# Cosformer attention and a token/channel mixer: first batch's u products moved two to three channel steps forward, one sine on ScalarE, half of a transpose copied

## The chip, the cores and the metric

The kernel runs on one core of a Trainium2 chip. The metric is device time in microseconds (us), the median of several runs. Five engines work beside each other, each in the order of its own instructions: TensorE (PE in the profile; its weight loads are PEld), VectorE (DVE), ScalarE (ACT), GpSimd (POOL) and SyncE (SP), which here only issues DMAs. An engine waits for another by a semaphore.

## The reference

For 8 batches, 8 heads, 576 positions and a head dimension of 64, the attention takes the positive part of q and k, multiplies each with the cosine and with the sine of its position's angle, and joins the two into 128 features. With these

```
kv  = sum over s of k_p[s,f] * v[s,d]          (per head)
z   = sum over s of k_p[s,f]
x   = (q_p @ kv) / (q_p . z + 1e-6)
```

The result, as x of shape 8 x 576 x 512, goes through a mixer:

```
h   = relu(x^T @ w_tok1) @ w_tok2              (over tokens, 576 -> 256 -> 576)
u   = x + h^T
out = u + relu(u @ w_ch1) @ w_ch2              (over channels, 512 -> 1536 -> 512)
```

Inputs and output are in 32 bits; products are taken in bf16.

## The kernel before

The 576 positions of a batch are four full chunks (0 to 3) of 128 rows and a tail of 64 rows, chunk `R` = 4. The tails of two batches share one tile of 128 rows: the even batch has rows 0 to 63, the odd batch rows 64 to 127 (`self.rows`).

A batch has a front and a channel part. The front (class `Front`) makes the features of k and q (`feature`, L246 to L264: relu of the input times cosine or sine, for 8 heads at once, on VectorE at L263 or on ScalarE at L261), copies v to bf16 (`values`, L276 or, on ScalarE, L274), sums kv (`kv`, L321), transposes q's features (`q_trans`, eight 128 x 128 transposes on TensorE and one copy of the result out of PSUM on ScalarE, L345; later batches use DMA transposes), forms x (`num`, L360 to L370), the token products (`tok1`, L383) and u (`tok2`: a pair of products of 512 columns at L407 and VectorE's add of x at L410).

The channel part (class `Channel`) has twelve steps `c_main` of four products of 512 columns (L552), each followed by an activation on ScalarE (L556), then the steps of the output, `o_step` (L585, two products of 512 columns each; the add at L590 and the store by SP follow when a chunk is full).

The loop at the end runs the steps of batch b's channel part, and between them the pieces of the next front. Which piece comes after which step is written out by hand: `pieces` returns a plan of (step, function, arguments), sorted by step, and pieces of one step stay in their order in the list. Nothing is rearranged later: each engine gets its instructions in this order. `KS` and `QS` in the plan are the cosine and the sine feature of a chunk of k or q (a last `True` puts the sine on ScalarE), `V` the copy of v, `KV` the kv products, `QT` the transposes of q, `N` is `num`, `u` is `tok2` of the batch before. `O` = 12 is the first output step.

The change is in the plan of batch 1 (`first`), whose pieces run between the channel steps of batch 0. Batch 0's u isn't needed for its channel steps: for this batch the turned u is made directly, and steps 0 to 2 have run already in `first_front` (L562), so that plan entries for steps 3 to 11 follow one `c_main` each. Its u is needed for the adds of the output steps, and its tail for the channel steps of the next batch.

GpSimd has, in this stretch, the copies of v's chunks 2 and 3, and three issues of the loads of `w_ch2` (`load_w_ch2`, L196) between and after them. The first output step needs the first third of `w_ch2`.

PSUM has two pools: `ps_mm`, four buffers of one bank, for the channel and output products among others, and `ps_at`, two buffers of two banks. A product into a buffer waits for the reader of what was there.

Of the kernel before, what the change touches and what calls it, by code (L numbers as in the profile page):

```python
# [16 lines left out]
def kernel(  # L17
# [15 lines left out]
    nc = tc.nc  # L33
# [7 lines left out]
    R = S // P  # L41
# [31 lines left out]
    ps_at = ctx.enter_context(tc.tile_pool(name="ps_at", bufs=2, space=bass.MemoryType.PSUM))  # L73
# [142 lines left out]
    class Front:  # L216
# [119 lines left out]
        def q_trans(self, ci, heads=(0, H), eng=nc.scalar, pool=ps_mm):  # L336
            lo, hi = heads
            qT_ps = pool.tile([P, hi - lo, P], BF16, name="qT_ps",
                              tag="mm" if pool is ps_mm else "at")
            for h in range(lo, hi):  # L340
                nc.tensor.transpose(qT_ps[:, h - lo, :],  # L341
                                    self.q_of(ci)[:, h, :, :].rearrange("p a b -> p (a b)"), ident)
            dst = self.qpT[:, ci * H + lo:ci * H + hi, :] if ci < R else self.tail.qpT[:, lo:hi, :]
            if eng is nc.scalar:
                nc.scalar.copy(dst, qT_ps)  # L345
            else:
                nc.vector.tensor_copy(dst, qT_ps)
# [114 lines left out]
        def pieces(self, b, before):  # L462

            first, odd, late = b == 1, b % 2 == 1, b == 2
            V, KV, N = self.values, self.kv, self.num
            KS, QS, QT, T = self.k_side, self.q_side, self.q_trans, self.tok2
            C, O = 0, NCH
            if first:  # L470

                u, act, pool = before.tok2, nc.scalar, nc.gpsimd
                plan = [(4, KS, 0), (4, KS, 1), (5, u, 0, ps_at, False), (5, KS, 2, True),
                        (6, KS, 3, True), (6, u, 1, ps_at, False), (7, KS, R), (7, V, R, nc.vector), (8, V, 0, act),
                        (8, V, 2, pool), (8, load_w_ch2, 0), (8, V, 3, pool),
                        (8, load_w_ch2, 1), (8, load_w_ch2, 2),
                        (8, u, 2, None, False), (9, V, 1, act), (9, u, 3, None, False),
                        (9, QS, 0), (10, u, R, None, False)]
                plan += [(11, KV, ci) for ci in range(NSC)]
                plan += [(11, QS, 1), (11, QS, 2), (11, self.kv_out),  # L480
                         (11, QT, 0, (0, H), act, ps_at), (11, QT, 1), (11, QS, R),
                         (O, QT, 2), (O, N, 0), (O, QS, 3), (O + 1, QT, R),
                         (O + 1, N, 1), (O + 3, N, 2), (O + 3, QT, 3),
                         (O + 5, N, R), (O + 7, N, 3), (O + 8, before.tail_cast)]
            else:
                if late:
                    plan = [(C + 5, V, 1, nc.vector), (C + 5, V, 3, nc.vector),
                            (C + 6, V, 0, nc.scalar), (C + 6, V, 2, nc.scalar),
                            (C + 7, V, R, nc.scalar)]
                else:  # L490
                    plan = [(C + at, V, ci, nc.scalar)
                            for ci, at in enumerate((-1, -1, 0, 1, 2))]

                if odd:
                    sides = ((-4, KS, 0), (-3, QS, 0), (0, KS, 1), (0, KS, 2), (1, QS, 1),
                             (1, KS, 3), (1, QS, 2), (2, QS, 3))
                elif late:
                    sides = ((-4, KS, 0), (-3, KS, 1), (0, KS, 2), (1, KS, 3), (1, QS, 0),
                             (2, QS, 1), (3, QS, 2), (4, QS, 3), (5, KS, R), (9, QS, R))
                else:  # L500
                    sides = ((-4, KS, 0), (-3, KS, 1), (0, KS, 2), (1, KS, 3), (1, QS, 0),
                             (2, KS, R), (2, QS, 1), (3, QS, 2), (4, QS, R), (5, QS, 3))
                for at, side, ci in sides:
                    plan.append((C + at, side, ci))
                    if side == QS:
                        plan.append((C + at, self.q_trans_dma, ci))

                plan += [(C + at, KV, ci) for ci, at in
                         enumerate((7, 7, 8, 8, 8) if late else
                                   (2, 3, 4, 5, 6) if odd else (2, 3, 4, 6, 7))]  # L510
                plan.append((C + (8 if late else 6 if odd else 7), self.kv_out))
            if first:
                at, mix, t = (), O + 7, O + 11
            elif odd:
                at, mix, t = (C + 8, C + 9, C + 10, C + 11, O + 2), O + 3, O + 7
            elif late:
                at, mix, t = (C + 10, C + 11, O + 1, O + 2, O + 4), O + 5, O + 9
            else:
                at, mix, t = (C + 9, C + 10, C + 11, O + 1, O + 3), O + 4, O + 8
            plan += [(i, N, ci) for i, ci in zip(at, ORDER)]  # L520
            plan += [(mix, self.mix_head, 0), (mix + 1, self.mix_head, 1),
                     (mix + 2, self.mix_tail)]

            plan += [(t + at, T, ci) for ci, at in enumerate((0, 1, 2, 3, 3) if not first else
                                                             (0, 0, 1, 2, 2))]
            plan += [(t + 3 - first, self.u_trans_dma, 3, R)]
            plan.append((t + 2 - first, self.u_trans_dma, 0, 3))
            if odd:
                plan.append((t + 3 - first, self.tail_trans_dma))
            slots = {}  # L530
            for slot, what, *args in sorted(plan, key=lambda p: p[0]):
                slots.setdefault(slot, []).append((what, args))
            return slots
# [281 lines left out]
```

## Time and profile before

| what | value |
|---|---|
| median of 3 runs | 268.99 us (268.74 to 269.48) |
| profiled execution | 268.4 us |
| its span | 266.6 us, 1.8 us less than its time |
| granted TensorE clock | 1.00 |
| busy TensorE, VectorE, ScalarE, GpSimd | 260.2, 166.1, 127.5, 12.3 us |
| channel steps 3 to 11 of batch 0 | 26.70 to 36.84 us |
| GpSimd in this stretch | 32.38 to 35.93 us |
| first output product (L585) | 38.96 us |

The span is what the profile shows, from the first to the last instruction; the time also holds what lies around it. Start times below are in us from the span's start. Matmuls are pipelined: a product's row is longer than the distance between two starts, and that distance, the pitch, is what tells whether TensorE waits. Features on VectorE overlap in the same way.

### The profile page before, as it was taken

Reading aid. Unit: us, or ns where it says so; the run is one execution under the profiler, and the core shown is the slowest. Engines: PE = TensorE matmul, PEld = TensorE weight load, DVE = VectorE, ACT = ScalarE, POOL = GpSimd, SP = SyncE. Lnnn points to the kernel's source line nnn. Section 1 sums busy time; section 2 is a strip of 40 time slices with the busy share of each in tenths; the row PEclk is TensorE's granted clock in tenths of the full one; section 3 lists DMA queues with packets and bytes.
Section 4 is the critical chain, followed back from the end, with each engine's and each line's share of the span. In section 5 each row is a group of like instructions: output and inputs, shape, how many; then the busy total and the mean of one; then the engine's idle time right before and its main releaser. Section 6 shows DMA issues by size and latency. Waiting matters only on the chain.

```text
span 266.6 us, 5133 instructions
## 1 busy us (share of the span) xinstructions
PE 260.2 (98%) x2042; PEld 139.9 (52%) x2063; DVE 166.1 (62%) x381; ACT 127.5 (48%) x224; POOL 12.3 (5%) x26
## 2 busy tenths in 40 slices
PE   7999999999999999999999999999999999999995
PEld 3675466465644455446644455446644455445544
DVE  6974699785665946785565846876565846720022
ACT  4953976428515461646515462546516362516500
POOL 6410130000000000000000000000000000000000
DMA  6999999779998999459984989289974580180022
GB/s 218 331 285 270 331 165 239 277 191 300 172 373 247 293 194 340 111 154 267 178 299 121 294 218 350 65 179 241 242 252 118 157 121 0 50 208 2 2 89 107
DMA packets 91959, 53.68 MB, mean 201 GB/s; under 512 B 59424, under 2 KB 87072, under 8 KB 91936
## 3 DMA queue, kind: packets, MB, share of 16 engines
q1 hardware_dynamic: 88576, 49.62, 70.0%
q0 software_dynamic: 2832, 3.21, 7.3%
q10 hardware_dynamic: 528, 0.52, 0.6%
q8 instruction: 16, 0.26, 0.4%
q14 instruction: 7, 0.06, 0.1%
HBM read 35.85 MB, written 9.44 MB: 170 GB/s over the span
## 4 chain that ended last, share of the span: by engine, by line
PE 86%; DVE 9%; DMA 2%; issue 1%; DVEq 0%
PE o_ps L585 34%; PE c_ps L552 25%; PE b_ps L383 6%; PE u_ps L407 6%; PE ct_ps L572 4%; PE kv_ps L321 3%; PE num_ps L360 3%; DVE x_sb L370 3%; DVE qp L263 2%; DMA qt<-in_q_dram 2%; PE idle_ps L204 1%; PE c_ps L562 1%; DVE u_sb L410 1%; PE qT_ps L341 1%; DVE den L368 1%
## 5 line engine op out<-in xcount | busy, mean ns | idle before, releaser
L585 PE MATMUL o_ps<-w_ch,h1T 128*128 128x512 bf16 (+2 forms) x392 | 92.7, 366 | 0.6
L552 PE MATMUL c_ps<-uT,w_ch 128*128 128x512 bf16 (+2 forms) x384 | 91.9, 372 | 0.1
L556 ACT ACTIVATE h1T<-c_ps 128x512 bf16<-128x512 f32 x93 | 55.4, 598 | 60.0 <-PE c_ps L552 59.7
L585 PEld LDWEIGHTS <-h1T 128*128 128x128 bf16 x408 | 37.6, 98 | 39.4
L552 PEld LDWEIGHTS <-w_ch 128*128 128x128 bf16 x384 | 33.6, 97 | 29.8
L590 DVE TENSOR_TENSOR o_sb<-o_ps,u_sb 128x512 f32<-128x512 f32 (+2 forms) x34 | 22.4, 659 | 29.2 <-PE o_ps L585 27.2
L410 DVE TENSOR_TENSOR u_sb<-u_ps,x_sb 128x512 f32<-128x512 f32 x32 | 21.7, 689 | 5.8 <-PE u_ps L407 5.6
L414 ACT CAST u_bf<-u_sb 128x512 bf16<-128x512 f32 x28 | 17.2, 618 | 16.7 <-DVE u_sb L410 16.7
L407 PE MATMUL u_ps<-B,w_tok 128*128 128x512 bf16 x79 | 22.4, 379 | 0.2
L388 ACT ACTIVATE B<-b_ps 128x512 bf16<-128x512 f32 x8 | 4.8, 597 | 34.1 <-PE b_ps L383 34.1
L370 DVE TENSOR_TENSOR x_sb<-num_ps,den 128x512 bf16<-128x512 f32 x28 | 19.4, 691 | 1.0
L572 PEld LDWEIGHTS <-w_ch 128*128 128x128 bf16 x192 | 13.9, 98 | 8.7
L263 DVE TENSOR_SCALAR kp<-kt,cos_t 128x512 bf16<-128x512 f32 x32 | 15.2, 479 | 4.2 <-DMA kt<-in_k_dram 4.2
L383 PE MATMUL b_ps<-x_sb,w_tok 128*128 128x512 bf16 x63 | 17.7, 379 | 0.1
L572 PE MATMUL ct_ps<-uT_tail,w_ch 128*128 128x128 bf16 x192 | 16.9, 219 | 0.0
L263 DVE TENSOR_SCALAR qp<-qt,cos_t 128x512 bf16<-128x512 f32 (+1 forms) x35 | 15.8, 452 | 0.5 <-DMA qt<-in_q_dram 0.5
L263 DVE TENSOR_SCALAR qp<-qt,sin_t 128x512 bf16<-128x512 f32 (+1 forms) x35 | 15.8, 452 | 0.0
L274 ACT CAST v_aug<-vt 128x512 bf16<-128x512 f32 (+1 forms) x28 | 15.5, 584 | 0.1
L590 DVE TENSOR_TENSOR o_sb<-o_ps,u_tail 128x512 f32<-128x512 f32 x4 | 2.8, 692 | 19.0 <-PE o_ps L585 19.0
L332 DVE CAST kv_sb<-kv_ps 128x260 bf16<-128x260 f32 x8 | 3.4, 431 | 17.1 <-ACT kv_sb L332 15.9
L360 PEld LDWEIGHTS <-qpT 128*128 128x128 bf16 x256 | 11.5, 98 | 4.9 <-issue 0.7
L263 DVE TENSOR_SCALAR kp<-kt,sin_t 128x512 bf16<-128x512 f32 x28 | 13.4, 480 | 0.0
(94 smaller groups left out, 232.1 us busy)
## 6 DMA issues: line engine op xcount, KB each, us to landing
out_dram<-o_sb SPq DMA_DIRECT2D x31, 256.0 KB, 3.2
kt<-in_k_dram SPq DMA_DIRECT2D x7, 1024.0 KB, 6.9
vt<-in_v_dram SPq DMA_DIRECT2D x7, 1024.0 KB, 7.6
qt<-in_q_dram SPq DMA_DIRECT2D x7, 1024.0 KB, 9.1
w_ch<-in_moe_w_ch_dram POOLq DMA_DIRECT2D x4, 384.0 KB, 10.7
w_ch<-in_moe_w_ch_dram POOLq DMA_DIRECT2D x3, 512.0 KB, 8.0
out_dram<-o_sb SPq DMA_DIRECT2D x9, 128.0 KB, 2.3
qtt<-in_q_dram SPq DMA_DIRECT2D x8, 128.0 KB, 5.2
```

The lines of the kernel that those rows point to most:

```text
L263: nc.vector.tensor_scalar(o_ap, i_ap, scalar1=w, scalar2=0.0, op0=ALU.mult, op1=ALU.max)
L360: nc.tensor.matmul(num_ps[:, g, j * DP:j * DP + D1], self.qT_of(ci, h), self.kv_sb[g][:, j, 0:D1], start=True, stop=True)
L370: nc.vector.tensor_mul(self.x_of(ci)[rows].rearrange("p (g j d) -> p g j d", g=2, j=HH), nv[:, :, :, 0:D], den.to_broadcast([rows.stop - r ...
L383: nc.tensor.matmul(self.b1_ps[mi], w, self.x_of(ci), start=(ci == ORDER[0]), stop=(ci == ORDER[-1]))
L407: nc.tensor.matmul(u_ps, w_tok2[:, ki, ci * P:(ci + 1) * P], self.B1[:, ki, :], start=(ki == 0), stop=(ki == NT - 1))
L410: nc.vector.tensor_add(u, u_ps[rows], self.x_of(ci)[rows])
L414: nc.scalar.copy(self.ub[:, ci, :], u)
L552: nc.tensor.matmul(c_ps[:, lo:hi], w_ch1[:, ki, mi * P:(mi + 1) * P], uT[:, lo // P:hi // P, ki, :], start=(ki == 0), stop=(ki == NCC - 1))
L556: nc.scalar.activation(self.h1T[:, mi, :], c_ps, AF.Relu)
L572: nc.tensor.matmul(self.ct_ps[:, mi % R, :], w_ch1[:, ki, mi * P:(mi + 1) * P], self.tail.uT[:, ki, :], start=(mi % R == 0 and ki == 0), s ...
L585: nc.tensor.matmul(o_ps, h, w_ch2[:, ki, cols], start=ki == 0, stop=ki == NCH - 1)
L590: nc.vector.tensor_add(o_sb, o_ps, u)
```

## The change

In the plan of batch 1, the u products of batch 0's chunks 0 to 3 and their adds move from the places after steps 5, 6, 8 and 9 to those after steps 3, 4, 5 and 6, all four in `ps_at`; the tail's moves from step 10 to step 8, still in `ps_mm`. The k features of chunks 0 to 3 move behind the four u, from steps 4, 4, 5 and 6 to steps 6, 6, 6 and 7; the tail's k features move from step 7 to step 8. The sine of query chunk 2 goes to ScalarE. Apart from the plan, `q_trans` for the tail of an odd batch copies only the columns of that batch's 64 rows out of PSUM; the transposes are the same. GpSimd's and SP's instructions keep their order.

```
@@ q_trans
             dst = self.qpT[:, ci * H + lo:ci * H + hi, :] if ci < R else self.tail.qpT[:, lo:hi, :]
+            if ci == R and self.rows.start:
+                dst, qT_ps = dst[:, :, self.rows], qT_ps[:, :, self.rows]
             if eng is nc.scalar:
@@ pieces
                 u, act, pool = before.tok2, nc.scalar, nc.gpsimd
-                plan = [(4, KS, 0), (4, KS, 1), (5, u, 0, ps_at, False), (5, KS, 2, True),
-                        (6, KS, 3, True), (6, u, 1, ps_at, False), (7, KS, R), (7, V, R, nc.vector), (8, V, 0, act),
+                plan = [(3, u, 0, ps_at, False), (4, u, 1, ps_at, False), (5, u, 2, ps_at, False),
+                        (6, u, 3, ps_at, False), (6, KS, 0), (6, KS, 1), (6, KS, 2, True),
+                        (7, KS, 3, True), (8, u, R, None, False), (8, KS, R),
+                        (8, V, R, nc.vector), (8, V, 0, act),
                         (8, V, 2, pool), (8, load_w_ch2, 0), (8, V, 3, pool),
-                        (8, load_w_ch2, 1), (8, load_w_ch2, 2),
-                        (8, u, 2, None, False), (9, V, 1, act), (9, u, 3, None, False),
-                        (9, QS, 0), (10, u, R, None, False)]
+                        (8, load_w_ch2, 1), (8, load_w_ch2, 2), (9, V, 1, act), (9, QS, 0)]
                 plan += [(11, KV, ci) for ci in range(NSC)]
-                plan += [(11, QS, 1), (11, QS, 2), (11, self.kv_out),
+                plan += [(11, QS, 1), (11, QS, 2, True), (11, self.kv_out),
```

## The prediction

> **What bounds the kernel now.** I read the page's busy shares first, then the timeline of TensorE, VectorE and GpSimd around the edited steps, then the chain that ended last in that stretch.
>
> ```profile
> PE 260.2 (98%) x2042; PEld 139.9 (52%) x2063; DVE 166.1 (62%) x381; ACT 127.5 (48%) x224; POOL 12.3 (5%) x26
> ```
>
> A busy TensorE is not yet a TensorE at its peak, so its starts are compared next.
>
> ```profile
> 26.70 2.75 PE L552 MATMUL c_ps<-uT,w_ch 128*128 128x512 bf16 x12
> 29.29 0.38 PE L407 MATMUL u_ps<-B,w_tok 128*128 128x512 bf16 x1
> 29.72 1.03 PE L552 MATMUL c_ps<-uT,w_ch 128*128 128x512 bf16 x4
> ...
> 34.47 1.03 PE L552 MATMUL c_ps<-uT,w_ch 128*128 128x512 bf16 x4
> 35.55 0.59 PE L407 MATMUL u_ps<-B,w_tok 128*128 128x512 bf16 x2
> 35.98 1.02 PE L552 MATMUL c_ps<-uT,w_ch 128*128 128x512 bf16 x4
> 36.84 1.14 PE L321 MATMUL kv_ps<-v_aug,kp 128*128 128x65 bf16 x32
> 38.06 1.06 PE L341 MATMUL qT_ps<-ident,qp 128*128 128x128 bf16 x16
> 38.96 0.38 PE L585 MATMUL o_ps<-w_ch,h1T 128*128 128x512 bf16 x1
> ```
>
> Columns are start, duration, engine, line, operation, tiles, count. Twelve products in 2.59 us (26.70 to 29.29) are 0.216 each; a channel step (four) takes 0.864, a u pair 0.43 (29.29 to 29.72). Nine such steps and five pairs make 9.94, and 26.70 to 36.84 is 10.14: TensorE is fed without a break but for one hole of 0.2, ahead of the pair at 35.55, which a channel step from 34.47 would let start at 35.33. That pair reuses the PSUM bank of the u product whose add is the first of the two at 34.80, done at 35.49. (A count of 1 where the pitch says 2 is a missing record.) From 49 to 263 us the windows show it busy for 213.19 of 214.00. So moving its products can shorten the run by that 0.2 and little else, while a new wait lengthens it one to one.
>
> ```profile
> 32.44 0.83 DVE L263 TENSOR_SCALAR kp_tail<-ktt,cos_t 64x512 bf16<-64x512 f32 x1
> 33.20 0.83 DVE L263 TENSOR_SCALAR kp_tail<-ktt,sin_t 64x512 bf16<-64x512 f32 x1
> 33.95 0.82 DVE L276 CAST v_aug<-vtt 64x512 bf16<-64x512 f32 x1
> 34.80 1.29 DVE L410 TENSOR_TENSOR u_sb<-u_ps,x_sb 128x512 f32<-128x512 f32 x2
> ...
> 39.43 0.49 DVE L263 TENSOR_SCALAR qp_tail<-qtt,cos_t 64x512 bf16<-64x512 f32 x1
> ```
>
> ```profile
> 32.38 0.62 POOL L276 CAST v_aug<-vt 128x512 bf16<-128x512 f32 x1 [11.74 <-DMA vt<-in_v_dram]
> 32.94 0.77 POOL L196 DMA_DIRECT2D w_ch<-in_moe_w_ch_dram  x1
> 33.70 0.79 POOL L276 CAST v_aug<-vt 128x512 bf16<-128x512 f32 x1
> 34.44 1.49 POOL L196 DMA_DIRECT2D w_ch<-in_moe_w_ch_dram  x2
> ```
>
> ```profile
> 32.72 0.48 issue
> 33.20 0.21 DVE kp_tail L263
> 33.41 0.54 issue
> 33.95 0.82 DVE v_aug L276
> ```
>
> The same feature operation takes 0.49 at 39.43, with its successor 0.40 behind it, and 0.83 with a successor 0.76 behind it while GpSimd casts and issues its loads; the chain calls the excess "issue", a wait that no semaphore explains. The u adds (L410, from PSUM) keep 0.60 apart, also next to GpSimd's later issues. So VectorE's SBUF features pay 0.36 each (0.755 less 0.395) beside this GpSimd stretch. The Trainium skill (SBUF — State Buffer, "SBUF: two separate sides") says that the two engines share a port pair under an exclusive lock, held for a whole instruction, for VectorE's two-port modes; these rows agree, since the third operation ends 0.29 after the second cast (34.77 against 34.49).
>
> **The change, part by part.**
>
> *The u products.* The pairs of chunks 0 to 3 go behind channel steps 3, 4, 5, 6, and start at 27.56, 28.86, 30.15 and 31.45; that of the tail follows step 8, at 33.6. The stretch holds the same products, and the tail's pair no longer waits for an add, so the hole goes: step 11 could start at 35.77, 0.2 sooner. All four now use the two-buffer pool; each finds its buffer free, since the add of two pairs before ends 1.2 us earlier. Worth 0.2, if VectorE keeps up.
>
> *The adds.* VectorE can start one 0.63 after its pair's start (the o pair at 47.16, its add at 47.79). So the last of the four runs at 32.08 and frees VectorE at 32.69. VectorE was idle until 28.76 for k's load; the adds use 0.6 of that, but then wait 0.7 between each other for TensorE, and the eight k features (six on VectorE) are queued behind them, 28.76 becoming 32.69.
>
> *VectorE's queue from 32.69, nothing in its way.* Six features at 0.395: 35.06. The tail's add, 0.60: 35.66. Two tail features and the tail's cast at 0.40: 36.86. First query chunk, 0.79: 37.65; second: 38.44, done at 38.52; cosine of the third: 38.84. TensorE started query chunk 0 at 38.06 and chunk 1 at 38.51 and could now do so 0.2 sooner; chunk 1 would start at about 38.6, 0.1 later than before. The 0.2 is given back, and 0.1 with it.
>
> *The same queue beside GpSimd.* GpSimd's cast starts at 32.38, when v lands, before the first feature; the order of GpSimd is unchanged. So now three full features meet the cast, the issue and the second cast which three tail operations met before. I take their measured starts: 32.69, 33.20, 33.95, and the fourth at 34.69 where free running gives 33.88: 0.81 later. Two more GpSimd issues follow (34.44 to 35.93), next to which the trace has no feature. The nearest row is the issue of 32.94, during which the feature at 33.20 lost 0.36; the farther row is the four issues at 10.55 to 13.76, beside which features kept 0.40. I take 0.36 for each of the two, as the next features again come out of a block and alternate with GpSimd; bounds 0 and 0.72 together.
>
> *A new wait on TensorE.* In the built program channel step 11 takes the PSUM bank of the tail's u product, so it waits for that add, which stands behind all six features. Free running it ends at 35.74, in time for 35.77. With 0.81 it ends at 36.55, with 0.81 + 0.72 at 37.27: step 11 starts 0.6 or 1.3 later than at 35.98, and kv, the transposes and the first o products are queued behind it. That isn't added to the later wait: it only moves TensorE closer to it.
>
> *The sine moved to ScalarE.* It takes 0.395 off VectorE (counted) and puts 0.80 (the rows at 29.98) on ScalarE after its activation of 37.04 to 37.64, where it idled 0.63 before the kv copy at 38.26. That copy slips by 0.1 to 38.34 at most; its readers wait for VectorE's half at 38.98 anyway. 0.
>
> *Half of the tail's transposes copied.* 1.04 becomes about 0.6 (that line's smallest copies, 512 columns, start at 0.59). The copy ended at 42.47 and its reader started at 43.65; ScalarE then waited 0.52 for transposes. 0; nothing but that idle time grows.
>
> *SP and GpSimd queues* keep their order; q's load and the first third of w_ch2 keep their issue times.
>
> *Sum.* Query chunk 1 is ready at 38.52 + 0.81 + 0.72 = 40.05, and TensorE starts it at 40.1 in place of 38.51: 1.6 us late. Later readers (the kv copy, then the tail queries at 41.7 against 42.1) are in time. Nothing behind gives it back: the u sums, transposing DMAs and loads of the next batches are issued from what TensorE has done. The profiled execution took 268.4 with a span of 266.6, so 270.0 and 268.2. The median of the runs, 268.99, is 0.6 above it; I add to that: 270.6.
>
> **Rivals.**
>
> *The last two GpSimd issues don't hold VectorE* (for: the rows at 10.55; against: the one at 33.20). Only 0.81 remains: chunk 1 is ready at 39.33, started at 39.4, 0.9 late: 269.9.
>
> *VectorE isn't interrupted, and GpSimd starves instead.* The features then end at about 35.2 (blocked by the first cast only), and the first third of w_ch2 can be described only then rather than by 33.7. The shortest of its three loads took 5.9 from issue to landing, so it landed about 38.84, and the first o product starts at 38.96: no slack. It would land 1.5 late: 270.5. For: at 10.36 to 13.99 features ran at full pitch beside four issues, whose loads needed 10.7 to land against 8.0 here. Against: the first feature comes out of a block. The Trainium skill (SBUF — State Buffer, "SBUF: two separate sides", its box on VectorE blocking DMA) describes exactly this starving; the rows at 10.36 agree, those at 33.20 do not.
>
> *Not slower.* If GpSimd's casts fall elsewhere, or a full-height feature isn't held as the 64-row ones were, only the 0.1 stays: 269.1. It decides as long as the six features lose less than some 0.7 in all: below that the second query chunk is at most 0.8 late. For: no row shows a 128-row feature beside a GpSimd cast. Against: the rows at 32.44 to 34.77, and v's landing, which the change does not touch.
>
> *Faster, but hardly.* Were VectorE's features ready in time after all, the hole of 0.2 would be the whole gain, 268.8, which is inside what counts as same; more would need TensorE time that the change does not remove.
>
> **How the numbers follow.** A measurement of this kernel tells about 0.3% (0.8 us) from no change. Chances: forecast 0.45; the issues not holding 0.20; starving 0.12; not slower, the 0.2 gained among it, 0.20; faster by more 0.03. The second case lies at the boundary, so a third of it counts as same. Slower: 0.45 + 0.13 + 0.12 = 0.70; same 0.20 + 0.07 = 0.27; faster 0.03. The range runs from 269.1 (not slower) to 271.1: forecast plus 0.5, when a stall of GpSimd's own (each of its issues held up by a 0.27 feature) comes on top.
>
> **What would show it.** In the trace after: four L410 rows ahead of the first k feature, which starts near 32.7; several k features of 0.8 in place of 0.48 between 32.7 and 36; the first idle or stretched pitch of TensorE ahead of the last channel step (before: 35.98), then query chunk 1 near 40.1; from there every later start about 1.6 later than before, up to the end. k features at 0.48 throughout and an o product waiting for a DMA would speak for starving; step 11 at 35.8 and transposes by 38.1 would make the prediction wrong.

## The result, and the profile after

The changed kernel takes 270.46 us (median of 7 runs, 270.02 to 271.20) against 269.46 of the kernel before, run beside it: a ratio of 1.0045, 95% interval 1.0026 to 1.0063. It is slower, by 0.7 to 1.7 us. Twelve more runs on another occasion gave 270.45 against 269.17, 1.0050 (1.0032 to 1.0067). The profiled execution took 270.66 with a span of 268.5 (before: 268.4 and 266.6), at a granted clock of 1.00.

The busy shares have hardly moved: a loss of 0.4% cannot be found there.

```profile
PE 261.0 (97%) x2042; PEld 139.6 (52%) x2063; DVE 165.7 (62%) x380; ACT 127.4 (47%) x225; POOL 12.3 (5%) x26
```

The timeline of TensorE after, columns as before; what stands in brackets is the idle time ahead of the row and what ended it:

```profile
34.27 1.89 PE L554 MATMUL c_ps<-uT,w_ch 128*128 128x512 bf16 x8
36.80 1.02 PE L554 MATMUL c_ps<-uT,w_ch 128*128 128x512 bf16 x4 [0.64 <-DVE u_tail L412]
...
39.77 0.62 PE L341 MATMUL qT_ps<-ident,qp 128*128 128x128 bf16 x8 [0.17 <-DVE qp L263]
...
74.50 0.42 PE L362 MATMUL num_ps<-kv_sb,qpT_tail 128*128 128x65 bf16 x8 [0.36 <-DMA qpT_tail<-qp_tail]
```

The hole ahead of the tail's u pair is gone: steps 9 and 10 follow it at full pitch. In its place the last channel step waits for the tail's add, the second query chunk for its sine, and a third wait, which I had not forecast, stands almost 35 us later, ahead of the product at 74.50.

VectorE and GpSimd after:

```profile
32.92 0.53 DVE L263 TENSOR_SCALAR kp<-kt,cos_t 128x512 bf16<-128x512 f32 x1
33.37 0.82 DVE L263 TENSOR_SCALAR kp<-kt,sin_t 128x512 bf16<-128x512 f32 x1
34.11 0.72 DVE L263 TENSOR_SCALAR kp<-kt,cos_t 128x512 bf16<-128x512 f32 x1
34.76 0.47 DVE L263 TENSOR_SCALAR kp<-kt,sin_t 128x512 bf16<-128x512 f32 x1
35.15 0.99 DVE L263 TENSOR_SCALAR kp<-kt,cos_t 128x512 bf16<-128x512 f32 x2
36.06 0.68 DVE L412 TENSOR_TENSOR u_tail<-u_ps,x_tail 64x512 f32<-64x512 f32 x1
```

```profile
31.90 0.61 POOL L276 CAST v_aug<-vt 128x512 bf16<-128x512 f32 x1 [11.43 <-DMA vt<-in_v_dram]
32.46 0.76 POOL L196 DMA_DIRECT2D w_ch<-in_moe_w_ch_dram  x1
33.22 0.69 POOL L276 CAST v_aug<-vt 128x512 bf16<-128x512 f32 x1
33.87 1.66 POOL L196 DMA_DIRECT2D w_ch<-in_moe_w_ch_dram  x2
```

Read the starts, not the durations. Free, a feature follows the last one after 0.395. Here the distances are 0.45, 0.74, 0.65, 0.39 and, from 35.15 to the add at 36.06, 0.91 for two. The six take 3.14 in place of 2.37 and lose 0.77. The first is held by the end of GpSimd's first issue, the second by its second cast, the third by its second issue and the fifth by its third issue; the fourth runs free inside that third issue, and the sixth has nothing beside it. The chain of waits goes straight through them, and puts its only larger piece without a releaser between them:

```profile
32.31 0.69 DVE u_sb L412
33.01 1.50 DVE kp L263 x3
34.51 0.25 issue
34.76 1.39 DVE kp L263 x3
36.14 0.61 DVE u_tail L412
```

### The profile page after: what moved, and what is told of

It reads as the page before. It is cut to its first block, busy times and chain, and to the rows that moved or that the text cites. A ratio compares the mean times of both kernels' runs of the same rounds, so it can differ in the third digit from the quotient of the medians.

```text
span 268.5 us, 5134 instructions
## 1 busy us (share of the span) xinstructions
PE 261.0 (97%) x2042; PEld 139.6 (52%) x2063; DVE 165.7 (62%) x380; ACT 127.4 (47%) x225; POOL 12.3 (5%) x26
## 4 chain that ended last, share of the span: by engine, by line
PE 87%; DVE 8%; DMA 3%; issue 1%; ACT 0%; DVEq 0%
PE o_ps L587 33%; PE c_ps L554 26%; PE u_ps L409 6%; PE b_ps L385 6%; PE ct_ps L574 4%; PE kv_ps L321 4%; DVE x_sb L372 3%; PE num_ps L362 3%; DMA qt<-in_q_dram 2%; DVE qp L263 1%; PE idle_ps L204 1%; DVE kp L263 1%; DMA qpT_tail<-qp_tail 1%; PE qT_ps L341 1%; PE c_ps L564 1%
```

## The experiments

The kernel before ran beside each of them: 269.01 us beside `order_only`, `sine_copy`, `tail_bank` and `between` (34 runs), 269.01 again beside the next four (24 runs), and 269.17 beside `pe_hold` and `after_again` (23 runs). The diffs are cut to the lines that tell.

**Which part costs: the order alone, and the two small edits alone.** `order_only` is the changed kernel without the sine on ScalarE and the half copy; `sine_copy` is the kernel before with these two.

```
order_only, against the kernel after:
-                plan += [(11, QS, 1), (11, QS, 2, True), (11, self.kv_out),
+                plan += [(11, QS, 1), (11, QS, 2), (11, self.kv_out),
...
-            if ci == R and self.rows.start:
-                dst, qT_ps = dst[:, :, self.rows], qT_ps[:, :, self.rows]
```

> The new order of the u products and k features alone, with the sine of query chunk 2 on VectorE and the whole copy as before. Theory (VectorE's queue runs late because the k features stand behind four paced adds and beside GpSimd): the loss is all in the order, so about 1.0 to 1.5 us slower than before, within 0.4 of the changed kernel; channel step 11 waits near 36.8 for the tail's add, query chunk 1 starts near 39.8, and the third chunk's sine costs VectorE 0.4 more, which shows as a later kv copy. Rival (the sine on ScalarE, behind which the kv copy and the transposes' copies queue, is what costs): this kernel is within 0.3 us of before.

> The old order with only the sine on ScalarE and the half copy. Theory: within 0.3 us of before; VectorE reaches the kv copy 0.4 sooner, and nothing on TensorE waited for that; ScalarE's kv copy slips by 0.1. Rival (the sine on ScalarE costs): 1 us slower than before, with num waiting for ScalarE's copies.

Measured: `order_only` 270.11, ratio 1.0044 (1.0029 to 1.0058); `sine_copy` 269.25, ratio 1.0007 (0.9993 to 1.0021). The whole loss belongs to the new order; the two small edits are worth nothing that can be measured. In `order_only` the six features run from 32.98 to 36.37, 1.02 lost, step 11 starts at 37.09 after a wait of 0.88, and query chunk 1 at 40.07. In `sine_copy`, where k landed at 28.00 and not at 28.73, and v at 31.52 and not at 32.33, the hole of 0.2 is absent although the old order stands. It is absent in `pe_hold` below too, where k and v landed within 0.07 of before: the tail's pair starts at 35.48, right behind the step of 34.61. So the 0.2 that the change could have won stands in one of three profiles of the old order.

**Is it the PSUM bank?** `tail_bank` lets the tail's u pair use the other pool, so that step 11 need not wait for its add.

```
-                        (7, KS, 3, True), (8, u, R, None, False), (8, KS, R),
+                        (7, KS, 3, True), (8, u, R, ps_at, False), (8, KS, R),
```

> The changed kernel, with the tail's u product in the two-buffer pool, so that channel step 11 has no bank to wait for. Theory (the wait of step 11 only brings TensorE nearer to the wait for the query features): step 11 starts unhindered near 36.0 instead of 36.8, but query chunk 1 still starts near 39.8, since VectorE's queue is the same; time within 0.3 us of the changed kernel. Rival (the bank is the cause): 0.8 us of the loss comes back.

Measured: 270.53, ratio 1.0053 (1.0035 to 1.0072), no better than the change. Its TensorE:

```profile
34.20 2.75 PE L554 MATMUL c_ps<-uT,w_ch 128*128 128x512 bf16 x12
...
38.93 0.62 PE L341 MATMUL qT_ps<-ident,qp 128*128 128x128 bf16 x8 [0.52 <-DVE qp L263]
39.72 0.62 PE L341 MATMUL qT_ps<-ident,qp 128*128 128x128 bf16 x8 [0.17 <-DVE qp L263]
```

Twelve products without a break: step 11 no longer waits. The first query chunk does, for 0.52, and chunk 1 starts at 39.72 (after: 39.77). The wait named at step 11 is not the cause; VectorE's queue is, and the bank only decides where TensorE meets it.

**Is it the place of the features?** `between` keeps the early u pairs but puts the k features between their adds, ahead of GpSimd's stretch, and the tail's k features ahead of its u. The new lines of the plan:

```
+                plan = [(3, u, 0, ps_at, False), (4, KS, 0), (4, u, 1, ps_at, False), (5, KS, 1),
+                        (5, u, 2, ps_at, False), (6, KS, 2, True), (6, KS, 3, True),
+                        (6, u, 3, ps_at, False), (7, KS, R), (8, u, R, None, False),
                         (8, V, R, nc.vector), (8, V, 0, act),
```

> The changed kernel's early u products, but the k features between the adds, where VectorE waits for TensorE: u0, k chunk 0, u1, k chunk 1, u2, k chunks 2 and 3, u3. Theory: the full k features are done before GpSimd's casts start near 32 and keep their pitch of 0.40; only the tail's features meet the casts, as before; no wait for step 11 nor for the query chunks, and the hole of 0.2 before the tail's u pair is gone: 0 to 0.3 us faster than before, 1 us or more faster than the changed kernel. Rival (early products cost by themselves, by their buffers or by ScalarE's later activations): it stays as slow as the changed kernel.

Measured: 269.30, ratio 1.0013 (0.9997 to 1.0029). The loss is gone. VectorE:

```profile
29.02 0.48 DVE L263 TENSOR_SCALAR kp<-kt,cos_t 128x512 bf16<-128x512 f32 x1
29.41 0.48 DVE L263 TENSOR_SCALAR kp<-kt,sin_t 128x512 bf16<-128x512 f32 x1
...
31.80 0.87 DVE L263 TENSOR_SCALAR kp<-kt,cos_t 128x512 bf16<-128x512 f32 x2
```

The k features keep 0.40 from 29.02 to 32.6, and what meets GpSimd is again the 64-row tail (0.71 and 0.86). Faster than before it is not. The hole of 0.2 is gone, but the first output product could now start 0.06 sooner, at 38.90, and waits 0.18 for the first third of `w_ch2`, which landed at 39.04 (before: 38.87): the load had no slack. `between_load` issues that third ahead of GpSimd's casts, still only when v has landed.

```
-                        (8, V, 2, pool), (8, load_w_ch2, 0), (8, V, 3, pool),
+                        (8, load_w_ch2, 0), (8, V, 2, pool), (8, V, 3, pool),
```

> The kernel with the k features between the adds, and the first third of w_ch2 issued ahead of GpSimd's first cast instead of behind it. In the kernel without this its first o product waited 0.18 for that load. Theory: that wait goes, since the load is issued 0.5 sooner; no wait on TensorE from 26.7 to 44 over 0.1; 0 to 0.4 us faster than before, which is less than what the rounds can tell. Rival: the casts come later and the last chunks of kv wait for v.

Measured: 269.04, ratio 1.0008 (0.9993 to 1.0022). The load landed at 38.25 and the wait is gone; 0.2 us of TensorE is still too little to tell from no change. So neither version beats the kernel before.

**How much does GpSimd hold VectorE?** `issues_first` keeps the changed order, but has GpSimd issue its three loads first and cast afterwards; `no_pool_casts` also moves the two casts to ScalarE (and query chunk 2's sine back to VectorE), so that only issues are left beside the features; `no_pool_stretch` lets these issues go when k has landed, so that nothing is left beside them.

```
issues_first, against the kernel after (the first load waits for v):
-                        (8, V, 2, pool), (8, load_w_ch2, 0), (8, V, 3, pool),
-                        (8, load_w_ch2, 1), (8, load_w_ch2, 2), (9, V, 1, act), (9, QS, 0)]
+                        (8, load_w_ch2, 0), (8, load_w_ch2, 1), (8, load_w_ch2, 2),
+                        (8, V, 2, pool), (8, V, 3, pool), (9, V, 1, act), (9, QS, 0)]
no_pool_casts, against issues_first:
-                        (8, V, 2, pool), (8, V, 3, pool), (9, V, 1, act), (9, QS, 0)]
+                        (9, V, 1, act), (9, V, 2, act), (10, V, 3, act), (9, QS, 0)]
no_pool_stretch, against no_pool_casts: the first load waits for k in place of v
```

> The changed kernel, with GpSimd's three loads of w_ch2 issued first when v has landed (near 32), and its two casts of v after them (near 34 to 35.5). Theory A (casts and issues both hold VectorE's features): the features still lose some 0.8 in all, the first ones beside the issues at a pitch near 0.75, the later ones beside the casts; time within 0.4 us of the changed kernel. Theory B (only casts hold): pitch 0.40 up to about 34.1, then 0.7 for two or three features beside the casts; time 0 to 0.4 us better than the changed kernel. Rival (128-row features are slow at this place for a reason of their own): the same pitches at the same features as in the changed kernel, the second and third ones the slow ones.

> The changed kernel, with the casts of v's chunks 2 and 3 on ScalarE (after steps 9 and 10), the sine of query chunk 2 back on VectorE, and GpSimd left with the three issues alone, made when v has landed (near 32 to 34.2). Theory A (issues hold too): two features lose about 0.3 each instead of 0.8 in all; step 11 starts near 36.4 and query chunk 1 near 39.3; 0.3 to 0.6 us better than the changed kernel. Theory B (only casts hold): pitch 0.40 throughout, step 11 near 36.0 and query chunk 1 near 38.9; about 0.8 us better. Rival (GpSimd has nothing to do with it): features as slow as in the changed kernel, and no gain.

> As the kernel with GpSimd left with the issues alone, but they are made when k has landed (near 28.5 to 30.7), so GpSimd does nothing while the features run. Theory (the loss is the features' 0.8 beside GpSimd, and what the paced adds cost alone is 0.1): all six features at 0.40, the tail's add done near 36, step 11 not later than 36.1, query chunk 1 near 38.8, with at most 0.3 of waiting in all, unless v or q land later behind the earlier weights; time within 0.4 us of before. Rival (the four adds paced by TensorE cost most): step 11 still waits 0.5 or more.

Measured: 271.01, ratio 1.0082 (1.0064 to 1.0100), in 4 runs; 269.77, ratio 1.0033 (1.0017 to 1.0048), in 6; 270.07, ratio 1.0047 (1.0027 to 1.0068), in 9. VectorE in `issues_first`:

```profile
33.18 0.62 DVE L265 TENSOR_SCALAR kp<-kt,sin_t 128x512 bf16<-128x512 f32 x1
33.73 0.84 DVE L265 TENSOR_SCALAR kp<-kt,cos_t 128x512 bf16<-128x512 f32 x1
34.49 0.82 DVE L265 TENSOR_SCALAR kp<-kt,sin_t 128x512 bf16<-128x512 f32 x1
35.24 1.58 DVE L265 TENSOR_SCALAR kp<-kt,cos_t 128x512 bf16<-128x512 f32 x2
```

and in `no_pool_stretch`:

```profile
33.16 0.48 DVE L265 TENSOR_SCALAR kp<-kt,sin_t 128x512 bf16<-128x512 f32 x1
33.56 0.48 DVE L265 TENSOR_SCALAR kp<-kt,cos_t 128x512 bf16<-128x512 f32 x1
33.96 0.48 DVE L265 TENSOR_SCALAR kp<-kt,sin_t 128x512 bf16<-128x512 f32 x1
```

In the first, features and GpSimd's items alternate from 33.73 on, at 0.75 a feature, whether the item is an issue (until 35.04) or a cast: 1.57 lost, the most of all runs and twice what I expected. In the second every feature keeps 0.395 and nothing is lost.

The two kernels differ in more than GpSimd's work beside the features: the loads run earlier in the second, and ScalarE makes the casts. The ends of the single features settle which it is. Six profiles have k features of 128 rows beside GpSimd (after, `after_again`, `order_only`, `tail_bank`, `issues_first`, `no_pool_casts`). In them 23 features are held, and each ends 0.22 to 0.25 after the end of the issue beside it or 0.28 to 0.29 after the end of the cast beside it. Seven features run free inside an issue, and just these seven issues take 0.85 to 0.93, all others 0.75 to 0.77. So of a feature and an item side by side one waits for the other, and GpSimd's work is the cause.

`no_pool_casts` lies between: beside issues alone two of six features are held, by 0.14 each; step 11 starts at 36.17 and query chunk 1 at 39.14. That misses what I took for an issue, 0.36. The time of `no_pool_stretch` misses the 0.4 us of before within which I expected it, and decides nothing: step 11 waits for nothing there, but the loads let go earlier hold back those of the queries (VectorE waits 0.24 for the first, TensorE then 0.21 at query chunk 1 and 0.66 for the tail queries, whose load landed at 40.67), the kv products wait 0.43 for ScalarE's casts, and the late wait, of which more below, is at its largest, 1.24. It shows VectorE free, not what that is worth; that the time comes back with the features is shown by `between`.

**Is a delay given back, and what is the wait at 74.50?** `pe_hold` is the kernel before with six products of no use put ahead of the kv products (they also take a turn of `ps_at`'s two buffers); `after_again` is the changed kernel with a second profile.

```
+        def hold(self, times):
+            t = ps_at.tile([P, 2, 512], F32, name="hold_ps", tag="at")
+            busy(t[:, 0, :], times)
...
+                plan.append((11, self.hold, 6))
                 plan += [(11, KV, ci) for ci in range(NSC)]
```

> The kernel before, with nothing of the change, and six products of an identity by a 512-column operand of zeros (left unread) put on TensorE ahead of the kv products: 6 x 0.216 = 1.30 us of TensorE alone, at the place where the change delays it, while VectorE, ScalarE, GpSimd and the loads keep their times. My theory (a delay there lengthens the run one to one): kv at 38.1 in place of 36.84, query chunk 0 at 39.4, every later start 1.3 later, median about +1.3 (ratio 1.0045 to 1.005); no wait for the transposing DMA of the tail's queries near 73 us if that wait has its own cause in the loads, a wait of 0.4 or more there if it comes of the delay itself. Rival (something behind gives part of it back, an idle stretch or a clock effect): median +0.7 or less, ratio below 1.003.

> The changed kernel once more, unaltered, on the same chip and with a profile of its own. If its losses are the same from run to run: six k features of 3.1 to 3.4 us in all beside GpSimd, query chunk 1 about 1.0 to 1.6 later than in the kernel before, ratio 1.004 to 1.005; the wait for the transposing DMA near 74 us (0.36) present again. If that later wait is chance of one execution, it is absent and the last product lies 1.0 to 1.3 behind the kernel before's.

Measured: `pe_hold` 270.19, ratio 1.0044 (1.0024 to 1.0065), that is +1.2 us (0.65 to 1.75) for a delay of 1.23 at the kv products; `after_again` as given above. TensorE in `pe_hold`:

```profile
36.77 1.46 PE L204 MATMUL hold_ps<-zeros,ident 128*128 128x512 bf16 x6
38.07 1.14 PE L321 MATMUL kv_ps<-v_aug,kp 128*128 128x65 bf16 x32
...
74.50 0.42 PE L364 MATMUL num_ps<-kv_sb,qpT_tail 128*128 128x65 bf16 x8 [0.40 <-DMA qpT_tail<-qp_tail]
```

The rival (something gives part of it back, ratio below 1.003) is not excluded: the interval begins at 1.0024, though its middle lies above. And this profile has a late wait on top of the delay, so that the +1.2 isn't the price of the delay alone.

The late wait is there although neither the order nor VectorE's queue is that of the change, so it doesn't need them. TensorE's pitch at this product is stretched by 0.52, 0.61 and 0.56 in after, `after_again` and `pe_hold`, by 0.88 in `no_pool_casts` and in `issues_first`, and by 1.24 in `no_pool_stretch`, but only by 0 and 0.10 in `order_only` and `tail_bank`, which are as late; in the four profiles without a delay (before, `sine_copy`, `between`, `between_load`) by 0.05 at most. Followed back, the product waits for the transposing DMA of the tail queries. This DMA waits for two things: its place in SP's queue, behind three other transposes, and the tail queries' features, which wait for the second of their two loads. In before that load took 4.2 us from issue to landing and the three transposes 4.67, and the transposed queries came 0.17 ahead of their product. In `after_again` the load was what ended last (5.3). In after it was SP's queue: the three transposes took 5.19, the DMA followed 0.09 behind them, and its features had been done for 0.53. In `pe_hold` both end together (5.0 and 5.20). In `order_only` and `tail_bank` neither is slow (4.2 and 4.3; 4.66 and 4.75). Why loads and transposes take longer in some of the late executions stays open, and so does the 0.88 of `no_pool_casts`, where both were issued late rather than slow (4.0 at most; 4.61).

## Why the prediction was right

It said 270.6 with a range of 269.1 to 271.1; 270.46 and 270.45 were measured. The mechanism held: VectorE's features land beside GpSimd, are held, and TensorE waits for VectorE's queue. Two terms of the sum were too large, and a wait that it did not have stands behind them.

That 270.46 lies so near 270.6 is in part luck. The forecast adds 1.6 to 268.99; beside the change the kernel before ran at 269.46, so that the change cost 1.0 by the medians (0.7 to 1.7 by the ratio), and 1.3 on the other occasion. A base 0.5 higher made up for most of what the sum had too much.

**The u pairs and the hole.** They start at 27.79, 29.09, 30.38 and 31.68, the forecast plus the 0.23 by which the whole front of this execution is late (step 3 at 26.93). The hole is gone, and worth nothing, since TensorE runs into VectorE's queue behind it; nor is it there in every execution of the old order.

**The paced adds.** The last one ends its turn at 32.92 (forecast 32.69, plus that 0.23). The pacing alone costs TensorE nothing up to step 11: in `no_pool_stretch` the features are through at 35.14, where free running was forecast to end at 35.06.

**The features beside GpSimd.** Forecast: 0.81 for cast, issue and cast, and 0.36 for each of the two later issues. Both were mis-sized.

| run | first cast starts | first feature starts | lost by the first two features | by the other four |
|---|---|---|---|---|
| tail_bank | 31.86 | 32.85 | 0.43 | 0.38 |
| after | 31.90 | 32.92 | 0.40 | 0.37 |
| after_again | 32.06 | 32.93 | 0.55 | 0.38 |
| order_only | 32.20 | 32.98 | 0.64 | 0.38 |

The 0.81 was measured where the cast starts at 32.38, 0.06 ahead of the first feature that meets it. Here v landed sooner (31.85 after, 32.33 before) and the first feature came 0.23 later, so that the cast was over before it began, and only part of the issue was left for it to meet. I had called v's landing something "which the change does not touch"; true, but it wanders by itself (31.5 to 32.4 over the runs), and the loss goes with it. (The two columns of losses are starts compared with 0.395 a feature.) The later issues cost 0.38 together in place of 0.72, the same in four runs: 0.25 for the one that the third feature meets, nothing for the fourth feature, and 0.13 for the fifth. The upper bound, 0.36 each, is not wrong: `issues_first` has it, where the features are in step with the issues. The top of the range, 271.1, came from a stall of each of these issues by a feature of 0.27, a length for which the prediction names no row; an issue with a free feature inside it takes 0.10 to 0.18 more than the 0.75 of the others.

**The wait of step 11** came, 0.64 and 0.78 in the two profiles of the change, and is not added to the later one (`tail_bank`). Step 11 started at 36.80 and 36.95; the sum with both terms had put the end of the tail's add at 37.27.

**Query chunk 1** was forecast at 40.1 and started at 39.77 and 39.92 (40.07 in `order_only`). From 40.1: 0.76 less for the features, 0.23 more for the late front, and 0.20 more behind them, where the tail's add takes 0.70 and not 0.60 ahead of a feature, its cast 0.46 and not 0.40, and chunk 1's own row starts a little later than its features are ready. That makes 39.77.

**"Nothing behind gives it back"** fits the first delay: `pe_hold` is late by 1.23 and pays about that (0.65 to 1.75). It was incomplete. The profile of after starts its last product 1.87 later than that of before (265.06 against 263.19): 1.26 from here, 0.52 from the late wait and 0.1 elsewhere. The medians differ by 1.0 and 1.3 only, so that not all of what this pair of profiles shows belongs to the change: the profiled execution of before was a quick one, 268.4 against medians of 269.0 to 269.5. How often the late wait occurs in unprofiled executions can't be read from them.

**The small edits.** Half the copy took 0.58 (forecast about 0.6) and ScalarE's idle time ahead of its last copy grew from 0.52 to 1.21; the sine took 0.80. `sine_copy` can't tell both together from 0.

**The rivals.** Starving did not happen here: the first third of `w_ch2` landed at 38.26 and the first output product started at 40.22 unhindered. It does happen in this program. In `issues_first` and `no_pool_stretch` the first issue of `w_ch1`'s loads, at 10.0 and 10.1, took 4.58 and 3.62 beside VectorE features that ran without a break. In the other ten profiles it took 0.84; in nine of these VectorE had just sat idle for k's load, by 0.2 to 0.6. The load still landed at 19.1 and 18.8 (19.0 to 20.1 in the others). The issues do hold VectorE, if only for half of what I took. "Not slower" needed a loss below some 0.7, and the runs lost 0.77 to 1.02: it was nearer than its chance of 0.20 says, with v landing a few tenths sooner. The lock that the Trainium skill describes (SBUF — State Buffer, "SBUF: two separate sides"), one engine blocked for the other's whole instruction, agrees with the casts: the feature held by the second cast ends 0.28 after it (34.19 against 33.91). The fourth feature ran its 0.47 inside an issue of 0.93; there the issue looks to be the one that waited, as it took 0.18 longer than the 0.75 of an issue that held a feature.

## What to carry to other kernels

When an operation is moved on an in-order engine, look at what runs on the neighbouring engine at the time where it lands, not only at its own queue: the adds were moved where nothing held them, and pushed the features into the one stretch where something did. The semaphore named at the first wait (here the PSUM bank) may only be the place where a late queue is first noticed; take it away and the wait moves to the next reader. And a price read from one profile holds for its alignment: take what is left of the neighbour's instruction when the moved one meets it, not a fixed sum for each operation, and, where that hangs on a load's landing, give it the width by which that landing wanders.

## What was unexpected in the hardware

The holding of VectorE's SBUF features by GpSimd's DMA issues is not one price. It was 0.14 for a feature beside issues alone (`no_pool_casts`), 0.25 behind a cast (after), 0.36 for each of a row of features in step with them (`issues_first`), and 0 for the fourth feature of after. One reading gives all the held ones: the feature ends 0.22 to 0.25 after the issue, so it loses what is left of the issue when it starts, less a constant (0.39 left and 0.14 lost, 0.50 and 0.25, 0.60 and 0.37). The issue is held as well: the last one took 0.93 after, and 0.75 before, where an add from PSUM stood beside it, and one beside unbroken features took 4.58 (`issues_first`, at 10.0). What decides which of the two goes first was not found.
